# A blocked attention and feed-forward kernel: the second block's attention queued behind the first's, four weight pieces split without ScalarE, and one small operation moved

## The chip, the cores and the metric

The kernel runs on one core of a Trainium2 chip. Such a core has five engines with a queue each, in which instructions run in order: TensorE (PE, with its weight loads PEld), VectorE (DVE), ScalarE (ACT), GpSimd (POOL) and SyncE (SP), which here only issues DMAs. The metric is the device time of one execution in microseconds. A kernel is run several times and the median counts; one execution is recorded by the profiler, and all durations in the text come from it.

## The reference

Attention within chunks of 64 tokens (8 batches, 8 heads, 576 tokens, 64 dimensions), and behind it a feed-forward layer over all 4608 tokens with a parametric ReLU.

```python
scores = scale * np.matmul(q_c, k_c.transpose(0, 1, 2, 4, 3))
scores = scores - np.max(scores, axis=-1, keepdims=True)
attn = np.exp(scores)
attn = attn / (np.sum(attn, axis=-1, keepdims=True) + 1e-09)
x = np.matmul(attn, v_c)          # brought to 4608 x 512
h = x @ w_in                      # 512 -> 2048
g = np.maximum(h, 0.0) + alpha * np.minimum(h, 0.0)
out = g @ w_out                   # 2048 -> 512
```

q, k, v and alpha are float32. The two weight matrices come to the kernel as 64-bit words: they are float64 numbers, and the kernel makes float32 of them with integer operations.

## The kernel before, in words

**Tiling.** A *sub-block* s is 128 tokens: two attention chunks with all 8 heads. There are 36. A *block* b is four sub-blocks (512 tokens). The hidden dimension is cut into 16 *chunks* f of 128. Each chunk has two weight *pieces*, wi[f] and wo[f], of 128 x 512 numbers. Every float32 operand of the feed-forward is split into a high part (the rounded matmul type) and a low part, and three products are added (high with high, low with high, high with low). So the first product of a chunk, `ffn_in` (L305, matmuls at L311), is 12 matmuls of 512 columns, and the second, `ffn_out` (L328, matmuls at L336), is 12 as well.

**Order of phases.** Blocks 0 to 2 go through `ffn_in` and `ffn_out` chunk by chunk; later blocks, in pairs, by another scheme that the change doesn't touch. The first steps are ordered so that the weights need not all be there: phase 0 is block 0 with chunks 0 to 2, phase 1 is block 1 with chunks 0 to 8, phase 2 is block 0 with chunks 3 to 15, and so on (L384). The list `steps` (L462) has an entry n for each (phase, block, chunk).

**Attention of the first two blocks.** Sub-blocks 0 to 7 are "early". `attend(part, s)` (L387) does one of three parts. Part 0 is `attn_scores` (16 matmuls at L178 into a bank ps_a) and `attn_softmax`: on VectorE a maximum (L208) and a scaling (L210), on ScalarE eight exponentials (L215, each with the reading of its sum), then on VectorE L217, a reciprocal (L218) and a multiplication (L219). Part 1 is `attn_transpose`: four transposes on TensorE (L243) and two copies on ScalarE (L250, L251). Part 2 is `attn_values` (16 matmuls at L261) and `attn_x`: ScalarE copies the high part, xh (L293), VectorE makes the low part, xl (L294). `ffn_in` reads the xh and xl of all four sub-blocks of its block, so it starts when the last of them is there. For s below 6 the transposes and the results of part 2 lie in the banks ps_o0 to ps_o3, in which `ffn_out` later sums; for s of 6 and 7 they lie in the two banks ps_a.

**Where it is called.** The parts of sub-blocks 0 to 3 are called in a loop ahead of the steps (L451). Those of sub-blocks 4 to 7 are put into `beside[n]` (L463) and called at the head of the first three steps (L820). All of them carry a raised priority.

**Weight pieces.** `fetch` (L115) loads one piece, 512 KB, into one of three buffers, from SP's queue. `split_weight` (L121) makes a float32 number of each 64-bit word and splits it. L130 takes the sign off the high words on ScalarE (every second 32-bit word is read). L131 to L134 clamp, shift and join on VectorE. L135 writes the high part on ScalarE, and L136 the low part on VectorE. `prepare(f)` (L139) does both pieces of a chunk: chunk 0 ahead of the attention loop, every further chunk in a step. `prepare(f, behind)` puts the instructions that stand on the engine of `behind` after it in that engine's queue. The dictionary at L827 names it: for chunk 2 the low part xl of sub-block 4 (`done_x[4]`), for chunk 3 that of 6, for chunk 4 that of 7.

**What sets the order.** The program order is not the order on an engine. A planner goes through the instructions with their priorities and a model of their durations, and writes each engine's queue at build time; on the chip the queue runs in that order. `tc.issue_after(ins)` fixes one thing for the planner: what is issued within it on the engine of `ins` comes behind `ins` in that engine's queue. It holds nothing on other engines. From step 20 on TensorE's order is the program's own.

**rise.** L448 makes 1 - alpha on VectorE from a small load on POOL's queue (L447). `prelu` (L301) reads it at L303, after the first `ffn_in`.

Of the kernel before, what the change touches and what calls it, by code (L numbers as in the profile page):

```python
# [11 lines left out]
AF = mybir.ActivationFunctionType  # L12
ALU = mybir.AluOpType
# [14 lines left out]
def tile_local_attention_prelu_ffn(  # L28
# [12 lines left out]
    nc = tc.nc  # L41
# [11 lines left out]
    SPB = TB // P  # L53
# [19 lines left out]
    def f32(t):  # L73
        return t.bitcast(F32)
# [31 lines left out]
    def pe(ins):  # L106

        return tc.keep_in_program_order(ins) if pinned[0] else ins

    wi, wo = {}, {}  # L110
# [7 lines left out]
        raws[side, f] = stage.tile([P, 512], I64, name=name, bufs=2 if name == "raw" else 1)  # L118
        nc.sync.dma_start(out=raws[side, f], in_=(w_in if side == "wi" else w_out)[:, f])

    def split_weight(side, f):  # L121
        if (side, f) not in raws:
            fetch(side, f)
        raw = raws.pop((side, f))
        words = raw.bitcast(U32).rearrange("p (n two) -> p two n", two=2)
        low, high = words[:, 0], words[:, 1]
        t1 = stage.tile([P, 512], U32, name="t1")
        w = const.tile([P, 2, 512], F32R, name=f"{side}{f}")
        hi, lo = w[:, 0], w[:, 1]
        nc.scalar.activation(f32(t1), f32(high), AF.Abs)  # L130
        nc.vector.tensor_scalar(f32(t1), f32(t1), bits(0x38000000), bits(0x47EFFFFF), op0=ALU.max, op1=ALU.min)  # L131
        nc.vector.tensor_scalar(t1, t1, 3, 0x3FFFFFF8, op0=ALU.logical_shift_left, op1=ALU.bitwise_and)
        nc.vector.scalar_tensor_tensor(t1, in0=high, scalar=0xC0000000, in1=t1, op0=ALU.bitwise_and, op1=ALU.bitwise_or)
        nc.vector.scalar_tensor_tensor(t1, in0=low, scalar=29, in1=t1, op0=ALU.logical_shift_right, op1=ALU.bitwise_or)  # L134
        nc.scalar.copy(hi, f32(t1))  # L135
        nc.vector.tensor_tensor(lo, f32(t1), f32(hi), op=ALU.subtract)  # L136
        return w

    def prepare(f, behind=None):  # L139
        with tc.issue_after(behind.ins) if behind else nullcontext():  # L140
            wi[f] = split_weight("wi", f)
            wo[f] = split_weight("wo", f)


    att = []
# [108 lines left out]
    def attn_values(s):  # L254
        v_sb = qkv.pop(s)[2]
        p = pdiag.pop(s)
        if s < EARLY:
            xo = attn_psum(s, 2)
            for h in range(H):
                par, hp = h % 2, h // 2  # L260
                pe(nc.tensor.matmul(  # L261
                    xo[par * C:(par + 1) * C, hp * P:(hp + 1) * P],
                    lhsT=v_sb[:, h * C:(h + 1) * C],
                    rhs=p[:, :, h],
                    start=True, stop=True,
                ))
            return xo.rearrange("p (g t) -> p g t", t=P)
# [10 lines left out]
                    ))  # L278
        return [a[:, :NP * C].rearrange("p (g t) -> p g t", t=C) for a in att]

    done_x = {}

    def attn_x(s, xo):
        sl = slice((s % SPB) * P, (s % SPB + 1) * P)
# [5 lines left out]
            return  # L290
        xh, xl = x[s // SPB]
        if s < EARLY:
            nc.scalar.copy(xh[:, :, sl], xo)  # L293
            done_x[s] = nc.vector.tensor_tensor(xl[:, :, sl], xo, f32(xh[:, :, sl]), op=ALU.subtract)  # L294
            return
        for c in range(2):
# [148 lines left out]
    first_v(2)  # L445
    fetch("wi", 1)
    nc.gpsimd.dma_start(out=alpha_sb, in_=alpha)  # L447
    nc.vector.tensor_scalar(rise, alpha_sb, -1.0, 1.0, op0=ALU.mult, op1=ALU.add)  # L448
    prepare(0)
    ready = 1  # L450
    for i in range(SPB + 2):  # L451
        for st in range(2, -1, -1):
            if 0 <= i - st < SPB:
                attend(st, i - st)
                if st == 2 and i % 2:
# [2 lines left out]
                    first_k(i + 2, nc.sync)  # L458
                    first_v(i + 1)


    steps = [(p, b, f) for p, (b, f0, f1) in enumerate(phases) for f in range(f0, f1)]  # L462
    beside = [[] for _ in steps]  # L463
# [336 lines left out]
    for n, (p, b, f) in enumerate(steps):  # L800
# [17 lines left out]
                    dst, src = finals.pop(0)  # L818
                    nc.sync.dma_start(out=dst, in_=src)
        for st, s in beside[n]:  # L820
            attend(st, s)
        if 2 * n in late:
            if 2 * n == visits[0]:
                attn_load(late[2 * n][1], "q")
            visit(*late[2 * n])
        if ready < NF:
            prepare(ready, done_x.get({2: SPB, 3: SPB + 2, 4: SPB + 3}.get(ready)))  # L827
            ready += 1
        elif n in COMBINE:

            with tc.issue_after(stages["softmax"][0].ins), tc.issue_after(stages["softmax"][1].ins):
                combine(*combined.pop(0), 23 <= n <= 36)
# [79 lines left out]
```

## Time and profile before

| what | value |
|---|---|
| median of 3 runs | 832.8 us (831.98 to 834.33) |
| the profiled execution: its own time | 834.16 us |
| its span, first to last instruction | 832.4 us |
| mean granted TensorE clock | 0.993 of full speed |

The profile counts from the span's start. A row of the timeline gives start, duration, engine, line, operation, output and inputs. "x16" says that 16 of a kind are merged in a row, and a bracket names the idle time ahead of it and what ended it. A row of groups gives count, busy us and mean ns of one. Names such as wo or wi in attention rows are the memory that the tile is kept in: before the weights of the last chunks are loaded, their room serves the attention's buffers.

### The profile page before, as it was taken

Reading aid. Unit: us, or ns where it says so; the run is one execution under the profiler, and the core shown is the slowest. Engines: PE = TensorE matmul, PEld = TensorE weight load, DVE = VectorE, ACT = ScalarE, POOL = GpSimd, SP = SyncE. Lnnn points to the kernel's source line nnn. Section 1 sums busy time; section 2 is a strip of 40 time slices with the busy share of each in tenths; the row PEclk is TensorE's granted clock in tenths of the full one; section 3 lists DMA queues with packets and bytes.
Section 4 is the critical chain, followed back from the end, with each engine's and each line's share of the span. In section 5 each row is a group of like instructions: output and inputs, shape, how many; then the busy total and the mean of one; then the engine's idle time right before and its main releaser. Section 6 shows DMA issues by size and latency. Waiting matters only on the chain.

```text
span 832.4 us, 15117 instructions
## 1 busy us (share of the span) xinstructions
PE 805.4 (97%) x5248; PEld 644.8 (77%) x5248; DVE 656.0 (79%) x1177; ACT 465.8 (56%) x1276; POOL 212.4 (26%) x340
## 2 busy tenths in 40 slices
PE   4799999999999999999999999999999999999998
PEld 3568788777777778787888787777887878888886
DVE  5687999987967988577788997777789956668875
ACT  5974565546563756565566554655465533345452
POOL 4006232323433322111112241111122512121232
PEclk9899999999999999999999999999999999999999
DMA  9729889556876767688876899786567995555788
GB/s 279 216 78 326 276 274 321 173 159 203 217 238 155 239 215 255 224 253 272 262 246 201 236 249 330 252 277 202 189 195 247 244 297 182 189 190 186 237 228 234
DMA packets 73964, 192.39 MB, mean 231 GB/s; under 512 B 11664, under 2 KB 19104, under 8 KB 73760
## 3 DMA queue, kind: packets, MB, share of 16 engines
q0 software_dynamic: 38272, 127.43, 49.8%
q1 hardware_dynamic: 27248, 48.91, 18.8%
q10 hardware_dynamic: 8368, 15.08, 5.9%
q8 instruction: 42, 0.69, 0.4%
q14 instruction: 34, 0.28, 0.1%
HBM read 135.27 MB, written 42.99 MB: 214 GB/s over the span
## 4 chain that ended last, share of the span: by engine, by line
PE 84%; DMA 6%; ACT 4%; DVE 4%; issue 1%; SPq 1%; POOL 0%; DVEq 0%; ACTq 0%
PE ps_o L624 19%; PE ps_o L757 15%; PE ps_o L336 12%; PE ps_h L311 12%; PE ps_h L757 12%; PE ps_h L624 9%; PE ps_a L273 2%; PE ps_a L192 1%; DMA raw<-w_in 1%; DMA pT<-t 1%; DMA wi<-qT 1%; DMA more<-w_in 1%; DMA wo_a<-raw 1%; ACT pr L215 1%; SPq L233 1%
## 5 line engine op out<-in xcount | busy, mean ns | idle before, releaser
L336 PE MATMUL ps_o<-wo,gh 128*128 128x512 f32 x384 | 116.4, 396 | 0.1
L311 PE MATMUL ps_h<-xh,wi 128*128 128x512 f32 x384 | 106.1, 400 | 2.6 <-ACT xh L293 2.3
L311 PEld LDWEIGHTS ps_h<-xh,wi 128*128 128x128 f32 x384 | 71.6, 189 | 20.3 <-ACT xh L293 2.5
L336 PEld LDWEIGHTS ps_o<-wo,gh 128*128 128x128 f32 x384 | 71.7, 188 | 17.5 <-ACT gh L323 0.3
L336 PE MATMUL ps_o<-wo,gl 128*128 128x512 f32 x192 | 71.2, 396 | 0.0
L624 PE MATMUL ps_o<-wi,raw 128*128 128x512 f32 x171 | 68.4, 400 | 0.0
L215 ACT ACTIVATE pr<-ps_a,mx 128x64 f32<-128x64 f32 x224 | 67.2, 325 | 0.7
L624 PE MATMUL ps_o<-wo,raw 128*128 128x512 f32 x171 | 67.3, 394 | 0.0
L311 PE MATMUL ps_h<-xl,wi 128*128 128x512 f32 x192 | 53.1, 397 | 0.0
L562 POOL DMA_DIRECT2D raw<-wi_a x42 | 22.3, 532 | 105.1 <-PE ps_o L624 61.8
L215 ACT ACTIVATION_READ_ACCUMULATOR pr<-ps_a,mx 128x1 f32 x224 | 48.8, 218 | 0.0
L302 ACT ACTIVATE wo<-gh 128x512 f32<-128x512 f32 x24 | 15.2, 633 | 52.0 <-DVE gh L647 52.0
L562 POOL DMA_DIRECT2D raw<-wo_a x42 | 22.3, 532 | 84.7 <-PE ps_o L757 43.9
L323 ACT CAST gh<-g 128x512 fp32r<-128x512 f32 x48 | 29.9, 624 | 24.1 <-DVE g L303 15.2
L311 PEld LDWEIGHTS ps_h<-xl,wi 128*128 128x128 f32 x192 | 36.3, 190 | 8.9 <-issue 0.2
L336 PEld LDWEIGHTS ps_o<-wo,gl 128*128 128x128 f32 x192 | 36.0, 188 | 8.7 <-issue 0.2
L580 ACT CAST gh<-wi 128x512 fp32r<-128x512 f32 x45 | 28.0, 622 | 26.2 <-PE ps_o L757 9.3
L324 DVE TENSOR_TENSOR gl<-g,gh 128x512 fp32r<-128x512 f32 x48 | 32.8, 684 | 8.8 <-ACT gh L323 8.5
L302 ACT ACTIVATE g<-ps_h 128x512 f32<-128x512 f32 x48 | 29.2, 608 | 18.8 <-PE ps_h L311 18.7
L303 DVE SCALAR_TENSOR_TENSOR g<-g,rise,ps_h 128x512 f32<-128x512 f32 x48 | 35.6, 741 | 5.0 <-ACT g L302 5.0
L624 PE MATMUL ps_o<-wi,wo 128*128 128x512 f32 x99 | 39.4, 398 | 0.0
L624 PE MATMUL ps_o<-wo,wo 128*128 128x512 f32 x99 | 39.2, 396 | 0.0
(247 smaller groups left out, 2154.6 us busy)
## 6 DMA issues: line engine op xcount, KB each, us to landing
raw<-wi_a POOLq DMA_DIRECT2D x42, 512.0 KB, 4.6
raw<-wo_a POOLq DMA_DIRECT2D x42, 512.0 KB, 4.6
wi<-wi_a POOLq DMA_DIRECT2D x21, 512.0 KB, 4.6
wo<-wi_a POOLq DMA_DIRECT2D x21, 512.0 KB, 4.6
wi<-wo_a POOLq DMA_DIRECT2D x21, 512.0 KB, 4.6
wo<-wo_a POOLq DMA_DIRECT2D x21, 512.0 KB, 4.3
v_sb<-v SPq DMA_DIRECT2D x28, 256.0 KB, 5.1
wi_a<-raw POOLq DMA_DIRECT2D x28, 256.0 KB, 3.5
```

The lines of the kernel that those rows point to most:

```text
L215: last = nc.scalar.activation(pr[:, g], one, AF.Exp, bias=mx[:, g], scale=SCALE, accum_out=sm[:, g])
L273: pe(nc.tensor.matmul(att[c][par * C:(par + 1) * C, hp * C:(hp + 1) * C], lhsT=v_sb[rows, h * C:(h + 1) * C], rhs=p[rows, :, par * NP + hp ...
L302: nc.scalar.activation(g, h, AF.Relu, scale=-1.0)
L303: nc.vector.scalar_tensor_tensor(g, in0=g, scalar=rise[:, f:f + 1], in1=h, op0=ALU.mult, op1=ALU.add)
L311: pe(nc.tensor.matmul(hps, lhsT=wi[f][:, l, k * P:(k + 1) * P], rhs=xx[:, k], start=(i == 0 and k == 0), stop=(i == 2 and k == NK - 1),))
L323: nc.scalar.copy(gh, g)
L324: low = nc.vector.tensor_tensor(gl, g, f32(gh), op=ALU.subtract)
L336: pe(nc.tensor.matmul(o, lhsT=a[:, ts], rhs=wo[f][:, l], start=(f == first and i == 0), stop=(f == last and i == 2),))
L562: streamed[0] = nc.gpsimd.dma_start(out=f32(t), in_=units[side][n])
L580: hi = nc.scalar.copy(t_hi, t)
L624: pe(nc.tensor.matmul(ps, lhsT=w[:, l, k * P:(k + 1) * P], rhs=xx[:, xl], start=first and at == 0, stop=at == n - 1, skip_group_check=not ...
L757: pe(nc.tensor.matmul(ps[m], lhsT=w[:, l, m * P:(m + 1) * P], rhs=xx, start=i != 6 and j == 0 and n == 0, stop=j == JF - 1 and n == 2, ski ...
```

## The change

Four things are done.

1. `split_weight` gets an argument `alone`, true for chunks 0 and 1. With it the sign is taken off by a bitwise AND on VectorE in place of ScalarE's Abs, and the high part is written by a copy on VectorE in place of ScalarE's. The four pieces of these chunks then need no ScalarE.
2. `attn_x` keeps ScalarE's copy in `copied_x[s]`, and `attn_values` its last matmul in `valued[s]`. All parts of sub-blocks 4 to 7 are issued behind `copied_x[3]` on ScalarE and behind `valued[3]` on TensorE, which are the first block's last.
3. The operation for `rise` moves from ahead of `prepare(0)` to after the first attention loop, behind `done_x[0]` on VectorE. Its load stays.
4. `prepare(2)` stands behind `done_x[3]` in place of `done_x[4]`.

```diff
-    def split_weight(side, f):
+    def split_weight(side, f, alone):
...
-        nc.scalar.activation(f32(t1), f32(high), AF.Abs)
+        if alone:
+            nc.vector.tensor_scalar(t1, high, 0x7FFFFFFF, None, op0=ALU.bitwise_and)
+        else:
+            nc.scalar.activation(f32(t1), f32(high), AF.Abs)
...
-        nc.scalar.copy(hi, f32(t1))
+        if alone:
+            nc.vector.tensor_copy(hi, f32(t1))
+        else:
+            nc.scalar.copy(hi, f32(t1))
...
-            wi[f] = split_weight("wi", f)
-            wo[f] = split_weight("wo", f)
+            wi[f] = split_weight("wi", f, f < 2)
+            wo[f] = split_weight("wo", f, f < 2)
...
-                pe(nc.tensor.matmul(
+                valued[s] = pe(nc.tensor.matmul(
...
-            nc.scalar.copy(xh[:, :, sl], xo)
+            copied_x[s] = nc.scalar.copy(xh[:, :, sl], xo)
...
-    nc.vector.tensor_scalar(rise, alpha_sb, -1.0, 1.0, op0=ALU.mult, op1=ALU.add)
     prepare(0)
...
+    with tc.issue_after(done_x[0].ins):
+        nc.vector.tensor_scalar(rise, alpha_sb, -1.0, 1.0, op0=ALU.mult, op1=ALU.add)
...
         for st, s in beside[n]:
-            attend(st, s)
+            with tc.issue_after(copied_x[SPB - 1].ins), tc.issue_after(valued[SPB - 1].ins):
+                attend(st, s)
...
-            prepare(ready, done_x.get({2: SPB, 3: SPB + 2, 4: SPB + 3}.get(ready)))
+            prepare(ready, done_x.get({2: SPB - 1, 3: SPB + 2, 4: SPB + 3}.get(ready)))
```

(`SPB`, sub-blocks per block, is 4.)

2 lines of the change are left out of this document (1 added, 1 removed).

## The prediction

> **What bounds the kernel now.** I read the page first, then the busy time by stretches, then the chain of waits of the first 80 us.
>
> ```profile
> span 832.4 us, 15117 instructions
> ...
> PE 805.4 (97%) x5248; PEld 644.8 (77%) x5248; DVE 656.0 (79%) x1177; ACT 465.8 (56%) x1276; POOL 212.4 (26%) x340
> ```
>
> TensorE is busy 805.4 of 832.4 us, so only 27 us of idle time can be won without taking matmuls away, and the change takes none away. The stretches of 20 us (sums of PE, PEld, DVE, ACT, POOL busy, then the granted clock) show where those 27 us lie.
>
> ```profile
> 0.00:20.00 20.00, 9.26 (x88) 7.35 (x88) 10.51 (x26) 10.48 (x44) 9.00 (x21) 1.00 0.94 280
> 20.00:40.00 20.00, 13.63 (x126) 10.94 (x128) 15.24 (x35) 19.47 (x85) 0.00 (x0) 0.83 0.78 234
> 40.00:60.00 20.00, 18.89 (x124) 14.04 (x118) 16.19 (x34) 14.01 (x46) 0.00 (x0) 1.00 0.17 54
> ...
> 240.00:260.00 20.00, 17.61 (x128) 14.04 (x128) 11.38 (x25) 12.49 (x50) 2.96 (x4) 0.91 0.61 170
> ```
>
> The first 40 us hold 17.1 us of it (20 - 9.26 and 20 - 13.63). In the second of these stretches ScalarE is busy 19.47 of 20: there it is the bound, not TensorE. The chain of waits (start, duration, engine, line) says what ends this stage.
>
> ```profile
> 28.02 1.49 ACT wo L215 x10
> ...
> 33.31 1.48 ACT wo L215 x10
> ...
> 36.16 0.51 ACT wo L135
> 36.66 0.50 ACT xh L293
> ...
> 37.20 2.12 PE ps_h L311 x8
> ```
>
> The first feed-forward matmul (L311) starts at 37.20, when the copy L293 of the first block's last sub-block is done. Ahead of that copy ScalarE runs softmax exponentials (L215) and weight pieces (L135). The first exponentials of sub-block 4, the second block's first, stand in the timeline here, and the copy of its last sub-block, 7, here:
>
> ```profile
> 27.88 0.36 ACT L215 ACTIVATE wo<-ps_a,mx 128x64 f32<-128x64 f32 x1
> ...
> 61.34 0.59 ACT L293 CAST xh<-ps_a 128x512 fp32r<-128x512 f32 x1
> ```
>
> So two sub-blocks of exponentials (4 and 5) that nobody needs yet go ahead of the copy that everybody waits for.
>
> **The change, part by part.** *ScalarE before the first feed-forward matmul.* These are the groups of ScalarE from 13.7 to 37.2 us that belong to weight pieces (count, busy us, mean ns), and one row of the timeline:
>
> ```profile
> L130 ACT ACTIVATE t<-raw 128x512 f32<-128x512 f32 x3 | 2.1, 694 | 0.0
> ...
> L135 ACT CAST wo<-t 128x512 fp32r<-128x512 f32 x2 | 1.3, 666 | 0.0
> ...
> L130 ACT ACTIVATE t<-more 128x512 f32<-128x512 f32 x1 | 0.7, 678 | 0.8 <-DMA more<-w_in 0.8
> L135 ACT CAST wi<-t 128x512 fp32r<-128x512 f32 x1 | 0.6, 643 | 0.0
> ```
> ```profile
> 32.63 0.67 ACT L130 ACTIVATE t<-raw 128x512 f32<-128x512 f32 x1
> ```
>
> The row at 32.63 is a piece of chunk 2, which stays on ScalarE. The other three L130 (2.1 us) and the three L135 (1.9 us) leave. Ten L215 rows, which are five exponentials with their sums, take 1.49 us, so 0.30 us each, and the 16 of sub-blocks 4 and 5 take 4.8 us; they go behind the copy. Together 8.8 us, and ScalarE has next to no idle time there, so the earliest start is 37.2 - 8.8 = 28.4 us.
>
> *What is late next is VectorE.* It takes over an AND and a copy for each of four pieces. The groups of VectorE (13.7 to 64.2 us) bound their price:
>
> ```profile
> L134 DVE SCALAR_TENSOR_TENSOR t<-raw,t 128x512 uint32<-128x512 uint32 x5 | 3.4, 687 | 0.0
> ...
> L131 DVE TENSOR_SCALAR t<-t 128x512 f32<-128x512 f32 x8 | 3.2, 422 | 0.7 <-ACT t L130 0.7
> ```
>
> Eight instructions at 0.42 (one source, like L131) are 3.4 us, at 0.69 (L134, which also reads every second word) 5.5 us. I take 0.42, since both have one source as L131 has, and keep 5.5 for the range. The Trainium skill ("VectorE: DVE Perf Modes", section "The perf-mode tier table (the rule you actually need)") gives fp32 copies and tensor_scalar in SBUF twice the rate of two-source operations, which the 0.42 against 0.69 here bears out for dense operands; no row here shows it for the strided AND. In return VectorE loses the wait of L448:
>
> ```profile
> DVE rise L448 <- DMA alpha_sb<-alpha: 1.2, 1, 1.2
> ```
>
> Now behind done_x[0], some 8 us later in the queue, it finds its load landed and costs nothing there; the 1.2 us came ahead of sub-block 0's reciprocal. Its DMA stays where it was on POOL's queue. Against this, VectorE's queue is in order, and an urgent reduction or reciprocal can stand behind a piece's 0.4 to 0.7 us. With some five such operations for each of sub-blocks 1 to 3, 15 in all, and every third of them behind 0.42 us of a piece, I take 2.1 us (bounds: nothing, and all 5.5 us). The start of L311 becomes 28.4 + 2.1 = **30.5**, 6.7 us earlier.
>
> *TensorE from there.* Rows of the timeline, and one of the chain (12 full matmuls):
>
> ```profile
> 30.58 1.09 PE L261 MATMUL ps_o<-wo,wi 128*64 128x128 f32 x16 [0.67 <-ACT wo L251]
> ...
> 34.26 0.66 PE L243 MATMUL ps_o<-ident,wo 128*128 128x128 f32 x4
> ...
> 61.36 2.14 PE L336 MATMUL ps_o<-wo,gh 128*128 128x512 f32 x8
> ```
> ```profile
> 235.21 2.81 PE ps_h L311 x12
> ```
>
> Phase 0 (block 0, chunks 0 to 2) is six groups of 12 matmuls: 16.8 us. The second block's attention is now wholly behind the start: four times 1.09 + 0.66 + 1.09 = 11.4 us. At best TensorE has done both at 30.5 + 28.2 = 58.7. In before the last group of phase 0 starts at 61.36 (L336) and is worth 2.8, so the same point is 64.2. The ceiling of the gain is 5.5 us, not 6.7, because three score groups and a transpose that lay in idle time now lie in the full stretch.
>
> *The added waits.* All of the second block's ScalarE instructions stand behind copied_x[3], its TensorE ones behind valued[3]. Behind those stand the prelu copies of block 0 on ScalarE, and, through PSUM banks ps_o0 to ps_o3 that sub-blocks 4 and 5 use, the first ffn_out. Until then TensorE has three ffn_in (8.4 us) and scores, so that wait is covered until some 41 us. What decides is when sub-block 7's copy (before: 61.34 + 0.59 = 61.9) lets phase 1 go on. Groups of ScalarE (37.1 to 64.2), and stretches:
>
> ```profile
> L323 ACT CAST gh<-g 128x512 fp32r<-128x512 f32 x3 | 1.9, 617 | 0.1
> ...
> L302 ACT ACTIVATE g<-ps_h 128x512 f32<-128x512 f32 x3 | 1.8, 599 | 3.5 <-PE ps_h L311 3.5
> ```
> ```profile
> 13.70:30.50 16.80, 11.95 (x110) 9.28 (x106) 13.00 (x34) 15.80 (x71) 0.00 (x0) 0.80 1.04 301
> 30.50:37.20 6.70, 3.65 (x52) 3.00 (x52) 4.61 (x12) 6.64 (x30) 0.00 (x0) 1.00 0.67 229
> 37.20:64.20 27.00, 25.62 (x164) 19.46 (x165) 22.01 (x45) 20.02 (x59) 1.42 (x3) 1.00 0.25 79
> ```
>
> VectorE worked 13.00 + 4.61 + 22.01 = 39.6 us from 13.7 to 64.2. Without chunk 3's two pieces (five operations of 0.42 to 0.69, some 2.9 us each, 5.8) and with the added 3.4 it needs 37.2; with the 3.8 us idle that it had up to 30.5, it is through at 13.7 + 37.2 + 3.8 = 54.7, with the dearer AND and copy at 56.8. ScalarE had less to do in the last stretch (20.02 against 22.01). So the copy can come at some 57 at the earliest. At the latest its chain keeps its old length from first exponential to last copy (61.9 - 27.9 = 34.0) from the new start: 64.5. I take the middle, **60.8**: half of the old chain's waits were for sub-block 0 to 3 and weight work that is now gone. TensorE goes on at 60.8 instead of 64.2: **3.4 us won**.
>
> *The rest.* prepare(2)'s VectorE part follows done_x[3] instead of done_x[4]: some 10 instructions, a sub-block earlier; its loads sit on SP's queue and aren't held. They compete with the second block on VectorE, which the 39.6 includes. On SP's queue the loads of values for 4 to 7 wait for TensorE's reads and only come earlier. From 64 us on TensorE is pinned or full, and the shift goes to the end. The 2.4 us idle in 240 to 260 may move by 1.5 us either way, which I cost at nothing and put into the range.
>
> **Sum.** Span 832.4 - 3.4 = 829.0; the profiled execution's own 834.16 becomes 830.8; it lay 1.4 above the median of the runs shown, 832.8, which becomes **829.4**.
>
> **Rivals.** *TensorE's ceiling:* the copy comes before 58.7 and all 5.5 us are won: 827.3. For it speak ScalarE's 20.02 and VectorE's 22.01 of 27 us; against it that both run in order behind one another. *The chain moves whole:* it keeps 34.0 us, ends at 64.5, and 0.3 is lost: 833.1.
>
> ```profile
> 41.47 0.24 ACT L215 ACTIVATION_READ_ACCUMULATOR wi<-ps_a,mx 128x1 f32 x1
> ...
> 52.33 0.32 ACT L215 ACTIVATE wi<-ps_a,mx 128x64 f32<-128x64 f32 x1
> ```
>
> For it speaks that from sub-block 6's last exponential to 7's first 10.6 us went by, while TensorE and VectorE worked through their queues and ScalarE was not the bound. That includes the case that the change doesn't do what it says: ScalarE's freed time fills with chunk 2's pieces. *Slower:* VectorE in the second block's softmax. Each added us there stretches the chain of 34.0; with all 3.4 to 5.5 us in it, the copy comes at 67.9 to 70.0, and the time is 3.7 to 5.8 longer: about 837.5. It decides once the copy comes later than 64.2. For it speaks 22.01 of 27 busy already, against it that four pieces can be split before 30.5 where 3.8 us are idle. *Half clock:*
>
> ```profile
> 20.00:25.00 5.00, 2.28 (x20) 1.88 (x22) 4.76 (x12) 4.96 (x25) 0.00 (x0) 0.71 1.05 284
> 25.00:30.00 5.00, 4.90 (x40) 3.83 (x36) 3.36 (x10) 4.99 (x25) 0.00 (x0) 0.60 1.03 299
> ```
>
> The granted clock is 0.71 and 0.60 after TensorE's idle time: 5 x 0.29 + 5 x 0.40 = 3.4 us lost. If that stretch falls on the new start, TensorE's end goes from 58.7 to 62.1, past 60.8, and 1.3 of the gain is lost: 830.7. The Trainium skill ("TensorE: Matmul & The Clock Gate", section "What's actually happening") has the clock halve after an idle window of about 3.4 us; by that rule one cold window would cost an estimated 1.7 us.
>
> **How the numbers follow.** Forecast 829.4 (own range 828.0 to 831.0): 0.35. Ceiling: 0.18. Whole chain: 0.24. Slower: 0.15. Half clock: 0.08. About 0.3%, 2.5 us, is what a measurement tells from no change: faster is below 830.3, slower above 835.3. Faster gets the ceiling and nearly all of the forecast, 0.53; slower 0.15, the rest is 0.32. The range goes from 826.0 (the ceiling and part of the later wait) to 835.5, which leaves out most of the slower case and little else.
>
> **What would show it.** L130 and L135 appear on ScalarE for chunks 2 and up only; L311 first at 29 to 32; sub-block 7's copy at 59 to 62; VectorE over 90% from 30 to 58; L448 without a wait. I am wrong if L311 starts after 34, if the AND or copy costs over 0.7, or if TensorE stands idle for over 4 us between 31 and 64.

## The result, and the profile after

The changed kernel is slower: 846.44 us (median, 843.52 to 847.09) against 832.39 us (831.89 to 834.33) of the kernel before beside it, a ratio of 1.0158 (95% interval 1.0128 to 1.0187). The forecast was 829.4, with a range up to 835.5. In the profiled executions the span grows from 832.4 to 845.1 us.

The line numbers of the changed kernel are some six higher: Abs is L133, ScalarE's cast of a piece L141, the new AND L131, the new copy L139, the scores L184, the maximum L214, the exponentials L221, xh L299, xl L300, `ffn_in` L317, `ffn_out` L342, prelu L308 and L309, rise L468.

| profiled execution | before | after | forecast |
|---|---|---|---|
| first `ffn_in` matmul | 37.20 | 33.96 | 30.5 |
| first exponential of sub-block 4 | 27.88 | 40.53 | 30.5 |
| first exponential of sub-block 6 | 39.24 | 50.20 | |
| sub-block 7's copy xh starts | 61.34 | 68.99 | some 60.2 (60.8 at its end) |
| span | 832.4 | 845.1 | 829.0 |

The added operations first. Groups of the changed kernel by line and shape, in its first 40 us (count, then busy us and mean ns of one, then the idle time ahead):

```profile
L131 DVE TENSOR_SCALAR t<-raw 128x512 uint32<-128x512 uint32 x3 | 1.3, 439 | 3.8 <-DMA raw<-w_in 3.4 <-DMA raw<-w_out 0.3
...
L139 DVE CAST wi<-t 128x512 fp32r<-128x512 f32 x2 | 0.9, 472 | 0.0
L139 DVE CAST wo<-t 128x512 fp32r<-128x512 f32 x2 | 0.8, 424 | 0.0
...
L468 DVE TENSOR_SCALAR rise<-alpha_sb 128x16 f32<-128x16 f32 x1 | 0.2, 170 | 0.0
```

They cost what they were put at: 0.42 to 0.47 us, and rise waits for nothing. The strided AND costs as little as the dense one-source row of before (0.44 against 0.42). The loss is in the order. Rows of the changed kernel's timeline (start, duration, engine; the bracket is the idle time ahead and what ended it):

```profile
32.63 0.67 ACT L133 ACTIVATE t<-more 128x512 f32<-128x512 f32 x1 [2.48 <-DMA more<-w_out]
...
33.33 0.58 ACT L299 CAST xh<-ps_o 128x512 fp32r<-128x512 f32 x1
33.94 0.69 DVE L300 TENSOR_TENSOR xl<-ps_o,xh 128x512 fp32r<-128x512 f32 x1 [3.52 <-ACT xh L299]
33.96 1.19 PE L317 MATMUL ps_h<-xh,wi 128*128 128x512 f32 x4 [0.87 <-ACT xh L299]
34.55 0.75 DVE L134 TENSOR_SCALAR t<-t 128x512 f32<-128x512 f32 x2
...
37.09 1.28 DVE L214 TENSOR_REDUCE mx<-ps_a 128x8 f32<-128x512 f32 x2
...
40.53 0.32 ACT L221 ACTIVATE wo<-ps_a,mx 128x64 f32<-128x64 f32 x1
...
45.13 1.09 PE L184 MATMUL ps_a<-wo,wi 128*64 128x128 f32 x16 [1.00 <-ACT wo L221]
...
50.20 0.32 ACT L221 ACTIVATE wi<-ps_a,mx 128x64 f32<-128x64 f32 x1
...
68.99 0.59 ACT L299 CAST xh<-ps_a 128x512 fp32r<-128x512 f32 x1 [1.19 <-PE ps_a L267]
...
69.62 3.54 PE L317 MATMUL ps_h<-xh,wi 128*128 128x512 f32 x8 [0.69 <-ACT xh L299]
...
79.67 1.69 PE L317 MATMUL ps_h<-xh,wi 128*128 128x512 f32 x4 [2.65 <-DVE g L309]
```

ScalarE stands idle for 2.48 us ahead of a piece of chunk 2 whose load isn't there, and sub-block 3's copy is queued behind it. VectorE waits 3.52 us for that copy, then does chunk 2's operations before it takes the second block's maxima (37.09). So sub-block 4's exponentials start at 40.53. Sub-block 6's scores (45.13) wait for exponentials: they use the bank that sub-block 4's scores held. Part of the lateness goes through to sub-block 7's copy: 12.7 us at sub-block 4's first exponential, 11.0 at sub-block 6's, 7.7 at the copy.

Up to 64 us TensorE hardly does less by it. Two stretches, 30 to 64 us, of the kernel before and then of the changed one (TensorE, weight loads, VectorE, ScalarE, GpSimd busy us, granted clock, DMA share, GB/s):

```profile
30.00:64.00 34.00, 29.07 (x215) 22.30 (x216) 26.92 (x57) 27.14 (x88) 1.22 (x2) 1.00 0.35 112
```
```profile
30.00:64.00 34.00, 28.41 (x200) 21.14 (x202) 16.84 (x37) 20.38 (x84) 0.00 (x0) 1.00 0.22 74
```

TensorE is busy for 28.41 us against 29.07. VectorE and ScalarE both do much *less*, 16.84 and 20.38 us of 34 against 26.92 and 27.14. Neither became the bound; they wait for each other.

How many feed-forward matmuls are done shows what this is worth. Windows restricted to one line, before: first the rows of `ffn_in` (L311), then those of `ffn_out` (L336); the figure in the first bracket is the number of matmuls.

```profile
0.00:64.00 64.00, 9.90 (x39) 7.36 (x40) 0.95 0.64 193
...
0.00:80.00 80.00, 20.21 (x81) 15.05 (x81) 0.96 0.70 217
...
0.00:64.00 64.00, 8.41 (x32) 5.78 (x32) 0.95 0.64 193
...
0.00:80.00 80.00, 14.91 (x59) 10.98 (x60) 0.96 0.70 217
```

The same of the changed kernel (L317, then L342):

```profile
0.00:64.00 64.00, 8.91 (x36) 6.64 (x36) 0.97 0.57 177
...
0.00:80.00 80.00, 16.63 (x61) 12.51 (x62) 0.96 0.59 187
...
0.00:64.00 64.00, 9.43 (x36) 6.46 (x36) 0.97 0.57 177
...
0.00:80.00 80.00, 9.43 (x36) 6.46 (x36) 0.96 0.59 187
```

By 64 us the two kernels are level: 39 + 32 = 71 and 36 + 36 = 72. The 72 are the whole of phase 0, six groups of 12. The changed kernel had a head start (24 against 8 at 40 us), but phase 0 holds no more work, and what comes next needs block 1's attention. By 80 us it is 140 against 97, 43 behind; at 0.234 us each (2.81 / 12, the chain's row of the prediction) that is 10.1 us. At 100 us the lag is 47, 11.0 us, and later it doesn't grow (47 at 140 us, 41 at 200).

Windows of the changed kernel at that place:

```profile
64.00:68.00 4.00, 1.64 (x22) 1.19 (x20) 2.25 (x6) 3.78 (x10) 0.00 (x0) 1.00 0.60 221
68.00:72.00 4.00, 3.31 (x22) 2.63 (x21) 4.00 (x9) 1.81 (x3) 0.08 (x1) 0.74 0.24 60
72.00:76.00 4.00, 4.00 (x16) 3.15 (x16) 2.84 (x6) 1.35 (x2) 4.00 (x6) 0.83 0.90 335
76.00:80.00 4.00, 1.35 (x6) 0.80 (x5) 3.97 (x8) 2.72 (x5) 4.00 (x6) 1.00 0.95 283
80.00:84.00 4.00, 4.00 (x12) 3.11 (x11) 2.15 (x5) 0.85 (x3) 3.20 (x5) 0.57 0.95 365
```

TensorE is busy for 1.64 of 4 us from 64, then runs at 0.74 and 0.83 of its clock, stands for 2.65 us until VectorE has made g (79.67), and runs at 0.57 after that. The clock alone costs up to 4 x (0.26 + 0.17 + 0.43) = 3.4 us from 68 to 84.

The Trainium skill ("TensorE: Matmul & The Clock Gate", section "What's actually happening") has the gate halve the clock after an idle window of about 3.4 us. The trace agrees that idle time is followed by the slower clock. The idle stretch ahead of the 0.57 is 2.65 us, though, shorter than that window.

### The profile page after: what moved, and what is told of

Its sections match the earlier page's. It is cut to its first block, busy times and chain, and to the rows that moved or that the text cites. A ratio compares the mean times of both kernels' runs of the same rounds, so it can differ in the third digit from the quotient of the medians.

```text
span 845.1 us, 15109 instructions
## 1 busy us (share of the span) xinstructions
PE 810.2 (96%) x5248; PEld 648.2 (77%) x5248; DVE 658.2 (78%) x1185; ACT 462.0 (55%) x1268; POOL 213.2 (25%) x340
## 4 chain that ended last, share of the span: by engine, by line
PE 75%; DMA 8%; DVE 7%; ACT 3%; SPq 3%; issue 2%; POOL 1%; DVEq 0%; ACTq 0%; POOLq 0%
PE ps_o L632 19%; PE ps_o L765 15%; PE ps_h L765 10%; PE ps_o L342 10%; PE ps_h L317 9%; PE ps_h L632 9%; SPq L239 3%; DMA pT<-t 2%; PE ps_a L279 1%; DMA wi_a<-raw 1%; DMA raw<-w_out 1%; PE ps_a L198 1%; DMA raw<-wi_a 1%; DMA more<-w_out 1%; DMA wo_a<-raw 1%
## 5 line engine op out<-in xcount | busy, mean ns | idle before, releaser
L342 PE MATMUL ps_o<-wo,gh 128*128 128x512 f32 x384 | 116.0, 397 | 1.0 <-DVE xl L300 1.0
L317 PE MATMUL ps_h<-xh,wi 128*128 128x512 f32 x384 | 108.4, 409 | 5.5 <-DVE g L309 3.9
L317 PEld LDWEIGHTS ps_h<-xh,wi 128*128 128x128 f32 x384 | 73.3, 194 | 24.3 <-DVE g L309 4.8
L342 PEld LDWEIGHTS ps_o<-wo,gh 128*128 128x128 f32 x384 | 71.6, 188 | 18.6 <-DVE xl L300 1.4
L342 PE MATMUL ps_o<-wo,gl 128*128 128x512 f32 x192 | 70.5, 395 | 0.0
L221 ACT ACTIVATE pr<-ps_a,mx 128x64 f32<-128x64 f32 x224 | 67.1, 324 | 0.7
L317 PE MATMUL ps_h<-xl,wi 128*128 128x512 f32 x192 | 55.8, 406 | 0.0
L570 POOL DMA_DIRECT2D raw<-wi_a x42 | 22.4, 532 | 105.4 <-PE ps_o L632 62.1
L221 ACT ACTIVATION_READ_ACCUMULATOR pr<-ps_a,mx 128x1 f32 x224 | 48.6, 217 | 0.0
L317 PEld LDWEIGHTS ps_h<-xl,wi 128*128 128x128 f32 x192 | 37.5, 195 | 9.1
L308 ACT ACTIVATE wo<-gh 128x512 f32<-128x512 f32 x24 | 15.2, 633 | 52.3 <-DVE gh L655 52.3
L342 PEld LDWEIGHTS ps_o<-wo,gl 128*128 128x128 f32 x192 | 36.1, 188 | 8.6
L588 ACT CAST gh<-wi 128x512 fp32r<-128x512 f32 x45 | 28.0, 621 | 26.3 <-PE ps_o L765 10.2
L309 DVE SCALAR_TENSOR_TENSOR g<-g,rise,ps_h 128x512 f32<-128x512 f32 x48 | 35.5, 740 | 7.0 <-ACT g L308 6.8
L632 PE MATMUL ps_o<-wo,wo 128*128 128x512 f32 x99 | 39.2, 396 | 0.0
L308 ACT ACTIVATE g<-ps_h 128x512 f32<-128x512 f32 x48 | 29.2, 608 | 17.6 <-PE ps_h L317 16.3
```

What stands on the lines that cost most here:

```text
L221: last = nc.scalar.activation(pr[:, g], one, AF.Exp, bias=mx[:, g], scale=SCALE, accum_out=sm[:, g])
L308: nc.scalar.activation(g, h, AF.Relu, scale=-1.0)
L309: nc.vector.scalar_tensor_tensor(g, in0=g, scalar=rise[:, f:f + 1], in1=h, op0=ALU.mult, op1=ALU.add)
L317: pe(nc.tensor.matmul(hps, lhsT=wi[f][:, l, k * P:(k + 1) * P], rhs=xx[:, k], start=(i == 0 and k == 0), stop=(i == 2 and k == NK - 1),))
L342: pe(nc.tensor.matmul(o, lhsT=a[:, ts], rhs=wo[f][:, l], start=(f == first and i == 0), stop=(f == last and i == 2),))
L570: streamed[0] = nc.gpsimd.dma_start(out=f32(t), in_=units[side][n])
```

## The experiments

Each kernel ran beside the kernel before on the same chip, whose median was 832.4 to 834.6 us, so ratios are compared. One table for all. The three times are starts in the profiled execution: sub-block 4's and 6's first exponential and sub-block 7's copy. The last column counts feed-forward matmuls by 80 us, as above.

| kernel | median | ratio to before (95%) | span | s4 | s6 | s7 | by 80 |
|---|---|---|---|---|---|---|---|
| before | 832.39 | | 832.4 | 27.9 | 39.2 | 61.3 | 140 |
| after | 846.44 | 1.0158 (1.0128 to 1.0187) | 845.1 | 40.5 | 50.2 | 69.0 | 97 |
| e1_chunk2_back | 840.87 | 1.0081 (1.0055 to 1.0108) | 839.3 | 38.6 | 47.4 | 65.4 | 116 |
| e2_no_hold | 836.90 | 1.0034 (1.0012 to 1.0057) | 839.3 | 27.7 | 38.6 | 67.2 | 118 |
| e3_pieces_back | 841.18 | 1.0088 (1.0061 to 1.0115) | 839.1 | 41.6 | 53.0 | 69.5 | 106 |
| e4_hold_alone | 839.26 | 1.0061 (1.0029 to 1.0093) | 836.4 | 38.1 | 47.0 | 65.0 | 120 |
| e5_pieces_alone | 833.77 | 0.9995 (0.9967 to 1.0022) | 833.9 | 28.3 | 37.3 | 61.8 | 135 |
| e6_chunk2_alone | 834.64 | 1.0008 (0.9985 to 1.0031) | 832.2 | 27.7 | 39.4 | 63.8 | 139 |
| e7_hold_scalar_only | 841.98 | 1.0091 (1.0066 to 1.0116) | 841.7 | 34.7 | 48.0 | 66.6 | 110 |
| e8_chunk2_last | 843.77 | 1.0125 (1.0053 to 1.0197) | 840.2 | 33.4 | 44.7 | 63.0 | 102 |
| h_s4 | 839.78 | 1.0071 (1.0045 to 1.0097) | 835.5 | 32.9 | 44.2 | 62.8 | 126 |
| h_s5 | 837.27 | 1.0026 (1.0006 to 1.0046) | 834.2 | 28.0 | 39.3 | 61.6 | 139 |
| best1 | 832.91 | 0.9991 (0.9963 to 1.0019) | 833.5 | 24.8 | 37.2 | 60.5 | 143 |
| o_rise | 834.70 | 1.0008 (0.9980 to 1.0035) | 829.7 | 28.7 | 40.0 | 62.1 | 137 |
| a_s4_free | 838.02 | 1.0049 (1.0026 to 1.0072) | 837.2 | 26.8 | 43.4 | 64.2 | 126 |
| best1_pool | 835.90 | 1.0024 (1.0002 to 1.0045) | 831.8 | 26.3 | 39.8 | 61.6 | 140 |

In the kernels that hold or move several sub-blocks, the exponentials of two of them can be interleaved; "s6" is then good to 2 us or so.

### One part of the change undone

**e1_chunk2_back**, the changed kernel with

```diff
-            prepare(ready, done_x.get({2: SPB - 1, 3: SPB + 2, 4: SPB + 3}.get(ready)))
+            prepare(ready, done_x.get({2: SPB, 3: SPB + 2, 4: SPB + 3}.get(ready)))
```

> The changed kernel, with chunk 2's pieces again behind the low part of sub-block 4 (done_x[4]) as before; all else as changed. Theory CHUNK (chunk 2's eight VectorE operations at 33.9 to 39.5 us stand ahead of the second block's reductions and scalings): the first exponentials of sub-block 4 come at 35 to 37 us instead of 40.5, sub-block 7's copy some 4 us earlier than 69.0, and the time falls by 4 to 9 us, to 837 to 842. Theory HOLD (the second block starts too late because everything of it stands behind the first block's last copy): sub-block 7's copy stays within 2 us of 69.0 and the time within 3 us of 846. Theory LOAD (VectorE has too much to do with the four pieces): no difference either.

**e2_no_hold**, the changed kernel with

```diff
-            with tc.issue_after(copied_x[SPB - 1].ins), tc.issue_after(valued[SPB - 1].ins):
-                attend(st, s)
+            attend(st, s)
```

> The changed kernel without the hold: the second block's attention is free on ScalarE and TensorE, as before; pieces on VectorE alone, the later 1 - alpha and chunk 2 behind done_x[3] stay. HOLD: the exponentials of sub-blocks 4 and 5 go into ScalarE's idle time between 20 and 33 us (9 us idle there in the changed kernel), sub-block 7's copy comes at 56 to 62, and the time is 829 to 834. CHUNK: chunk 2's pieces still stand ahead of work of the second block, so 838 or more. LOAD: 838 or more as well, since the pieces stay on VectorE.

**e3_pieces_back**, the changed kernel with

```diff
-            wi[f] = split_weight("wi", f, f < 2)
-            wo[f] = split_weight("wo", f, f < 2)
+            wi[f] = split_weight("wi", f, False)
+            wo[f] = split_weight("wo", f, False)
```

> The changed kernel with all weight pieces again split by ScalarE and VectorE together; hold, later 1 - alpha and chunk 2 behind done_x[3] stay. LOAD: eight operations of 0.43 us (3.4 us) leave VectorE and the time falls by 3 us or more, to 843 or less. HOLD and CHUNK: VectorE was not full between 40 and 64 us, so nothing is won; ScalarE gets six conversions of 0.65 back ahead of the first block's last copy, and the time is 844 to 850.

**e4_hold_alone**, the kernel before with the hold of sub-blocks 4 to 7 on ScalarE and TensorE only:

```diff
-            attend(st, s)
+            with tc.issue_after(copied_x[SPB - 1].ins), tc.issue_after(valued[SPB - 1].ins):
+                attend(st, s)
```

> The kernel before with nothing but the hold added: sub-blocks 4 to 7 behind the first block's last copy on ScalarE and its last matmul on TensorE. HOLD: sub-block 7's copy comes at 65 us or later and the time is 840 to 846. CHUNK: the hold alone costs little, 831 to 836. LOAD: as CHUNK.

Measured: without the hold 0.34% is left of the 1.58%; without the early chunk 2 0.81%, without the pieces on VectorE 0.88%. The hold by itself costs 0.61%. So the hold is the largest single part, but no part carries all of it. Against what was expected: e1 has CHUNK's time and earlier copy, but its exponentials came at 38.6, not at 35 to 37. e2 lies between the theories, above HOLD's 829 to 834 and below the others' 838. e3 has LOAD's 843 or less, though the pieces cost nothing alone (e5 below). e4 has HOLD's copy at 65.0, and its time lies 0.7 us under HOLD's 840 to 846.

Without the hold (e2) sub-block 6's exponentials are back at 38.6 us, yet sub-block 7's copy is still late. Rows of e2's timeline:

```profile
64.16 1.10 PE L267 MATMUL ps_a<-wi,wi 128*64 128x128 f32 x16 [0.32 <-ACT wi L257]
64.77 0.59 ACT L372 COPY wo<-ps_o 128x512 f32<-128x512 f32 x1
...
66.73 0.61 ACT L372 COPY wi<-ps_o 128x512 f32<-128x512 f32 x1
67.20 0.62 ACT L299 CAST xh<-ps_a 128x512 fp32r<-128x512 f32 x1
```

The values end at 65.3, but ScalarE's queue has four copies of block 0's sums (L372) and a piece's cast ahead of the urgent xh. The planner ordered them so; on the chip it costs 2 us. e2's profiled execution was also its slowest (841.12 against a median of 836.90), so its trace shows more loss than is usual for e2.

### Parts alone, and the hold on one engine

**e5_pieces_alone** and **e6_chunk2_alone** are the kernel before with one part each:

```diff
-            wi[f] = split_weight("wi", f)
-            wo[f] = split_weight("wo", f)
+            wi[f] = split_weight("wi", f, f < 2)
+            wo[f] = split_weight("wo", f, f < 2)
```
```diff
-            prepare(ready, done_x.get({2: SPB, 3: SPB + 2, 4: SPB + 3}.get(ready)))
+            prepare(ready, done_x.get({2: SPB - 1, 3: SPB + 2, 4: SPB + 3}.get(ready)))
```

> The kernel before with nothing but the four pieces of chunks 0 and 1 on VectorE alone; no hold, chunk 2 behind done_x[4], 1 - alpha early. LOAD (VectorE's added work costs by itself): slower than before by 3 us or more, 837 and up. RELIEF (ScalarE is the bound of the first 37 us and this frees it): the first block's last copy comes earlier than 36.5 us and the time is 829 to 833. ORDER (what each engine's queue comes to is what counts, and the freed time is filled with other work of the second block): the first copy not earlier than 36.5, the time 833 to 838.

> The kernel before with nothing but chunk 2 behind done_x[3] in place of done_x[4]. If chunk 2's early place costs by itself: 837 or more, with sub-block 7's copy at 64 us or later. If it costs only together with the hold, which puts the second block's reductions at that very place: 831 to 836 and the copy at 60 to 63, since sub-blocks 4 and 5 are reduced before 30 us here.

**e7_hold_scalar_only** is the changed kernel with the hold on ScalarE alone and chunk 2 back at `done_x[4]`; **e8_chunk2_last** is e7 with chunks 2 and 3 later:

```diff
-            with tc.issue_after(copied_x[SPB - 1].ins), tc.issue_after(valued[SPB - 1].ins):
+            with tc.issue_after(copied_x[SPB - 1].ins):
...
-            prepare(ready, done_x.get({2: SPB, 3: SPB + 2, 4: SPB + 3}.get(ready)))
+            prepare(ready, done_x.get({2: SPB + 2, 3: SPB + 3, 4: SPB + 3}.get(ready)))
```

> The changed kernel with the hold on ScalarE alone (TensorE free to make the second block's scores early) and chunk 2 behind done_x[4] again. If the hold costs by the scores and reductions that come late (TensorE's half of it): sub-block 4's exponentials start within 1.5 us of the first block's last copy, sub-block 7's copy comes before 61 us, and the time is 828 to 834. If it costs by ScalarE's idle time that can't be used: the copy still comes at 64 us or later and the time is 837 to 841, like the changed kernel with chunk 2 put back (840.9).

> As the run before this one, but chunk 2's VectorE part behind the low part of sub-block 6 and chunk 3's behind that of 7, so that no weight piece stands among the second block's softmax. LATE (the time follows sub-block 7's copy): the copy at 52 to 58 us and the time 826 to 832, the best of all. WEIGHTS (the pieces are then late for phase 0's third chunk and for phase 1): TensorE waits over 4 us for chunk 2, and the time is 834 or more.

Measured: the pieces and the early chunk 2 alone change nothing that can be told (0.9995 and 1.0008). In e5 sub-block 3's copy even comes at 41.36, later than before's 36.49, for the planner fills ScalarE's freed time with the second block's exponentials. The hold on ScalarE alone (e7) is as dear as that on both engines (1.0091 against e1's 1.0081, intervals overlapping), so the loss is not TensorE's hold. With TensorE free sub-block 4's exponentials do come 3.9 us earlier (34.7 against e1's 38.6), right behind sub-block 3's copy, but sub-block 7's copy doesn't (66.6 against 65.4). e8 takes the pieces out of the way: sub-block 4's exponentials come at 33.4, 7 us earlier than in the changed kernel, sub-block 7's copy at 63.0, and it still costs 1.25%. Two of e8's windows:

```profile
56.00:60.00 4.00, 1.09 (x4) 0.72 (x4) 2.58 (x7) 2.04 (x12) 0.00 (x0) 0.77 0.00 0
60.00:64.00 4.00, 3.02 (x19) 2.45 (x20) 3.90 (x8) 2.53 (x5) 0.00 (x0) 0.50 0.18 30
```

TensorE is dry there: by 56 us 48 of the 72 matmuls of phase 0 are done, by 64 only 51. Phase 0 now lacks chunk 2. The copy of sub-block 7 alone therefore does not tell the time; what TensorE has done by 80 us does.

Of the expectations, ORDER came for e5. e6 has the time of its second case (831 to 836), with the copy 0.8 us past that case's 63. e7 has the early exponentials of its first case, but the copy and the loss of its second, 1 us above that range. For e8 WEIGHTS came; LATE's copy at 52 to 58 didn't.

### Which sub-block's hold

**h_s4** and **h_s5** are the kernel before with the hold on ScalarE, and for one sub-block:

```diff
-            attend(st, s)
+            with tc.issue_after(copied_x[SPB - 1].ins) if s == SPB else nullcontext():
+                attend(st, s)
```

(h_s5 has `s == SPB + 1`.)

> The kernel before, with the hold on ScalarE alone (behind copied_x[3]) and for sub-block 4 alone; pieces, chunk 2 and rise as before. Theory (sub-block 4's bank): sub-block 4's exponentials come some 10 us later than before (35 to 39 in place of 28), its scores keep their ps_a bank until then, so sub-block 6's exponentials come at 44 or later (before 39.2) and sub-block 7's copy at 64 or later (before 61.3): 4 us or more slower, 837 to 841. Rival (idle ScalarE: what costs is ScalarE time that stays unused ahead of the first feed-forward matmul, whichever sub-block is held): half of what the whole hold costs, +2 to +3, 835 to 837, and sub-block 6's exponentials at 41 to 43. Rival (the hold costs by the cold TensorE only): the granted clock between 24 and 40 is below 0.7 and the time follows it, not the copy.

> The kernel before, with the hold on ScalarE alone and for sub-block 5 alone; sub-block 4 is free. Theory (sub-block 4's bank): sub-block 4's exponentials stay ahead of sub-block 3's copy at 27 to 31, sub-block 6's come at 39 to 42, sub-block 7's copy at 60 to 63; time 831 to 836, not over 0.3% from before. Sub-block 3's copy may come 1 to 4 us earlier than at 36.6. Rival (idle ScalarE): +2 to +3, 835 to 837, with sub-block 7's copy at 63 to 66. If sub-block 6's exponentials come at 44 or later here too, the bank that sub-block 5's scores hold does the same, and sub-block 4 is nothing special.

Rows of h_s4's timeline:

```profile
32.88 0.32 ACT L221 ACTIVATE wo<-ps_a,mx 128x64 f32<-128x64 f32 x1
...
37.80 1.10 PE L317 MATMUL ps_h<-xh,wi 128*128 128x512 f32 x4
...
38.83 1.09 PE L184 MATMUL ps_a<-wo,wi 128*64 128x128 f32 x16
...
44.23 0.31 ACT L221 ACTIVATE wi<-ps_a,mx 128x64 f32<-128x64 f32 x1
```

And of h_s5's:

```profile
28.02 0.34 ACT L221 ACTIVATE wo<-ps_a,mx 128x64 f32<-128x64 f32 x1
...
34.10 1.04 PE L184 MATMUL ps_a<-wo,wi 128*64 128x128 f32 x16
...
35.75 0.32 ACT L221 ACTIVATE wo<-ps_a,mx 128x64 f32<-128x64 f32 x1
...
39.28 0.31 ACT L221 ACTIVATE wi<-ps_a,mx 128x64 f32<-128x64 f32 x1
```

Holding sub-block 4 alone costs 0.71%, 5.9 us, as much as the whole hold (0.61%). Its profiled execution ran at a granted clock of 1.00 from 24 to 100 us and took 837.31 us. The kernel before beside it took 830.3 to 835.5 us, 833.8 on average, in its five executions with a mean clock of 0.998 or more. So some 3.5 us are lost without a slower TensorE clock. The rest of the 5.9 may be the clock's: four of h_s4's six executions, with means of 0.993 to 0.997, took 839.7 to 841.8. Of the theory's numbers sub-block 6's 44 or later and the time came; the exponentials of 4 (32.9 for 35 to 39) and sub-block 7's copy (62.8 for 64 or later) came earlier than it had them. Holding 5 alone costs 0.26%, at the edge of what can be told: sub-block 6's exponentials stay at 39.3, as the theory had it, but the time, 837.3, is over its 831 to 836 and at the rival's +2 to +3, though not with the rival's copy at 63 to 66 (it came at 61.6). In h_s4 sub-block 5's exponentials too run behind 4's (from 35.2), so it holds both in effect. One thing of the theory isn't borne out there: sub-block 6's scores don't wait for the bank in h_s4. They stand in TensorE's queue behind 24 matmuls of `ffn_in`, and sub-block 6's exponentials stand in ScalarE's queue behind the copies and casts of 4 and 5. The bank's wait itself shows only where TensorE is held as well: 1.00 us in the changed kernel (at 45.13), 1.60 in e3, 0.34 in e1 and e4; whether the planner put those scores late because of the bank wasn't tried.

**o_rise** is the kernel before with the later operation:

```diff
-    nc.vector.tensor_scalar(rise, alpha_sb, -1.0, 1.0, op0=ALU.mult, op1=ALU.add)
     prepare(0)
...
+    with tc.issue_after(done_x[0].ins):
+        nc.vector.tensor_scalar(rise, alpha_sb, -1.0, 1.0, op0=ALU.mult, op1=ALU.add)
```

> The kernel before with the later 1 - alpha alone. VectorE doesn't wait 1.2 us for alpha's load ahead of sub-block 0's reciprocal. All theories: no effect that lasts, as the first two blocks' end is set later; sub-block 7's copy at 60 to 63, time 831 to 836. If it is over 2.5 us slower, the later place of this operation is part of what the changed kernel loses, and the sums of the other parts must be taken again.

1.0008, no effect that can be told, as expected.

### Sub-block 4 free in the changed kernel, and two tries for a faster one

**a_s4_free**, the changed kernel with

```diff
-            with tc.issue_after(copied_x[SPB - 1].ins), tc.issue_after(valued[SPB - 1].ins):
-                attend(st, s)
+            if s == SPB:
+                attend(st, s)
+            else:
+                with tc.issue_after(copied_x[SPB - 1].ins), tc.issue_after(valued[SPB - 1].ins):
+                    attend(st, s)
```

> The changed kernel with one thing undone: sub-block 4 isn't held, neither on ScalarE nor on TensorE; sub-blocks 5 to 7 are, chunk 2 stands behind done_x[3], the pieces and rise as changed. Theory (sub-block 4's bank): its exponentials go back ahead of sub-block 3's copy (25 to 31), sub-block 6's come at 37 to 43 in place of 50.2, sub-block 7's copy at 59 to 64 in place of 69.0; 831 to 837. Rival (chunk 2's pieces: their VectorE operations ahead of the second block's reductions are worth some 5 us by themselves, as the changed kernel lost 5.6 us more than the one with chunk 2 put back): 838 to 842, and sub-block 6's exponentials at 44 or later. Rival (hold of sub-blocks 5 to 7): 843 or more.

Freeing this one sub-block takes the ratio from 1.0158 to 1.0049, some two thirds of the loss. Three rows of its timeline:

```profile
26.80 0.31 ACT L221 ACTIVATE wo<-ps_a,mx 128x64 f32<-128x64 f32 x1
...
38.19 1.28 DVE L214 TENSOR_REDUCE mx<-ps_a 128x8 f32<-128x512 f32 x2
...
41.02 0.32 ACT L221 ACTIVATE wo<-ps_a,mx 128x64 f32<-128x64 f32 x1
```

The exponentials of 4 are early again (26.80), but the maxima of 5 and 6 come at 38.19, behind chunk 2's pieces, and sub-block 7's copy at 64.15. The time, 838.0, is above the theory's range by 1 us and at the low end of the rival's. So sub-block 4's hold is the greater part of the loss. That the early chunk 2, which costs nothing alone, is part of what is left is what the maxima's place suggests.

**best1** keeps the pieces and rise as changed, holds sub-block 5 alone on ScalarE, and has chunk 2 back at `done_x[4]`:

```diff
-            with tc.issue_after(copied_x[SPB - 1].ins), tc.issue_after(valued[SPB - 1].ins):
+            with tc.issue_after(copied_x[SPB - 1].ins) if s == SPB + 1 else nullcontext():
                 attend(st, s)
...
-            prepare(ready, done_x.get({2: SPB - 1, 3: SPB + 2, 4: SPB + 3}.get(ready)))
+            prepare(ready, done_x.get({2: SPB, 3: SPB + 2, 4: SPB + 3}.get(ready)))
```

> The changed kernel with three things undone: sub-block 4 isn't held, the hold on TensorE is gone, and chunk 2 stands behind done_x[4] again. Left are the pieces of chunks 0 and 1 on VectorE alone, the later rise, and the hold of sub-block 5 on ScalarE. Theory (sub-block 4's bank): sub-block 3's copy at 33 to 36 and sub-block 7's at 59 to 63: 829 to 835, level with before or a little faster. Rival (idle ScalarE): with 8.8 us gone from ScalarE's queue more of it stays unused, 837 to 841, as with the hold and the pieces together (841 to 842).

**best1_pool** is best1 with a part of the pieces' work on GpSimd:

```diff
-        nc.vector.tensor_tensor(lo, f32(t1), f32(hi), op=ALU.subtract)
+        eng = nc.gpsimd if 3 <= f < 9 and side == "wo" else nc.vector
+        eng.tensor_tensor(lo, f32(t1), f32(hi), op=ALU.subtract)
```

> The kernel of best1 with the low part of the pieces wo of chunks 3 to 8 written by GpSimd in place of VectorE (six operations). best1 was 3 feed-forward matmuls ahead of before at 80 us and 1 behind at 100, where VectorE was busy 3.7 to 4 of 4 us. Theory (VectorE sets the pace from 80 to 100): six operations of 0.69 us leave VectorE's queue, 4 us in all, of which 0.5 to 2 us come through to TensorE: 829 to 833. Rival (GpSimd is late: its operation takes 2 us or more, and ffn_out of the chunk and the DMA issues behind it wait): 834 to 842.

best1 is level with before (0.9991), as its theory had it. It differs from e7 in one thing only, that sub-blocks 4, 6 and 7 aren't held, and e7 costs 0.91%. Sub-blocks 6 and 7 lie behind sub-block 3's copy in before too (39.24 against 36.49), so this leaves sub-block 4. best1 has sub-block 3's copy at 33.92 and sub-block 7's at 60.48, and is 3 matmuls ahead at 80 us, but 1 behind at 100 (223 against 224). best1_pool, 1.0024, is no better. Groups of its GpSimd and VectorE from 60 to 100 us, each from a view of its own engine:

```profile
L143 POOL TENSOR_TENSOR wo<-t,wo 128x512 fp32r<-128x512 f32 x5 | 7.7, 1544 | 60.1 <-ACT wo L141 60.1
...
L143 DVE TENSOR_TENSOR wi<-t,wi 128x512 fp32r<-128x512 f32 x5 | 3.7, 731 | 0.7 <-ACT wi L141 0.7
```

The subtraction takes 1.54 us on GpSimd against 0.73 on VectorE. Neither theory was borne out in full: TensorE is full in every window from 64 to 96 us, and the median still isn't lower. No kernel here beats the one before.

## Why the prediction was wrong

*Prices.* AND 0.44, copy 0.42 to 0.47, rise without a wait, L133 and L141 on ScalarE for chunks 2 and up only: as forecast. The early chunk 2 and the later rise cost nothing that can be told by themselves (e6, o_rise): right too. The pieces don't win anything either (e5), though the prediction took 4.0 us off ScalarE for them. One reading was off without harm: the 0.69 that it set against 0.42 for dense operands is L134's, which reads every second word; the dense subtraction L136 takes 0.69 too.

*Start of `ffn_in`: 30.5 forecast, 33.96 measured.* 3.2 of the 6.7 us came. The 8.8 us taken off ScalarE left room, but ScalarE's queue then had a piece of chunk 2 ahead of sub-block 3's copy, and waited 2.48 us for its load. But the load is not the only bound. Rows of e8, where the same piece waits for 0.55 us:

```profile
31.75 1.09 PE L267 MATMUL ps_o<-wi,wi 128*64 128x128 f32 x16 [1.26 <-ACT wi L257]
32.25 0.67 ACT L133 ACTIVATE t<-more 128x512 f32<-128x512 f32 x1 [0.55 <-DMA more<-w_out]
32.95 0.59 ACT L299 CAST xh<-ps_o 128x512 fp32r<-128x512 f32 x1
```

The copy starts 0.11 us after sub-block 3's last values are there (31.75 and 1.09). In h_s4 it starts at 32.40, 0.05 after them, with all pieces still on ScalarE; no run brings it earlier. So with the second block's exponentials out of the way the first block's own chain of transposes, copies and values sets the start. The prediction subtracted 8.8 us of ScalarE's work and didn't ask when that chain would be done.

*"At the latest its chain keeps its old length from first exponential to last copy (61.9 - 27.9 = 34.0) from the new start: 64.5."* **This step failed.** The length was no underestimate: from 40.53 to 69.58 (68.99 and 0.59) the chain took 29.1 us. Its start was wrong by 10 us, and part of that, 4.9 us, came back in a shorter chain. The prediction let sub-block 4's exponentials start with `ffn_in` at 30.5; they started 10 us later: behind the copy at 33.33, and behind maxima that came at 37.09, behind chunk 2's VectorE operations. Those operations had been counted as busy time ("which the 39.6 includes") and not as a place in an in-order queue: VectorE waited 3.52 us for the copy with chunk 2 lined up behind it, and the maxima behind that. In e1 chunk 2 is out of the way and the exponentials still start at 38.6, since the hold on TensorE puts the scores at 33.6 to 37.1 there; with that gone too they start right behind the copy (e7, 34.7). Their start alone is not the whole loss, for e7 still costs 0.91%. In before, the exponentials of 4 and 5 lay ahead of sub-block 3's copy from 27.9 to 36, in slots of ScalarE that the hold forbids. h_s4 shows that giving up these slots for sub-block 4, and in effect for 5, is enough for 5.9 us; best1, which gives up only 5's, loses nothing.

*"TensorE's ceiling" of 5.5 us.* It treated a head start as a gain. In e5 the first `ffn_in` matmul comes 4.8 us later than before, and the time is the same (0.9995):

```profile
42.00 2.13 PE L317 MATMUL ps_h<-xh,wi 128*128 128x512 f32 x8 [0.66 <-ACT xh L299]
```

So the start of `ffn_in`, which the prediction set out to move, doesn't set the time there. e8 and the changed kernel show the same: phase 0 is 72 matmuls, the changed kernel was 16 ahead at 40 us and level by 64, and from there only block 1's attention counts. That wait the prediction did count, at 60.8; it came at 69.6.

*What was missing in kind:* the price of a late copy. The prediction charged each microsecond of lateness once. The changed kernel's first matmuls of block 1 run at a lower clock (8 of them in 3.54 us; 8 at full clock take 2.12 in the prediction's chain), then TensorE waits 2.65 us for VectorE's g, and runs at 0.57 afterwards. Two windows of e3 at the same place:

```profile
76.00:80.00 4.00, 2.32 (x11) 1.87 (x11) 4.00 (x8) 2.70 (x5) 3.30 (x5) 1.00 1.03 403
80.00:84.00 4.00, 4.00 (x19) 3.25 (x18) 4.00 (x9) 2.24 (x5) 3.06 (x5) 1.00 1.01 376
```

TensorE waits less there, and the clock stays at 1.00. One reason may be that e3 still has 11 matmuls of phase 0 to do at 64 us (61 done against 72), which fill the wait for block 1. e3 is level with the changed kernel at 72 us (80 matmuls against 78) and 15 ahead at 88 (140 against 125); that difference, 3.5 us, comes after the late copy. That the cause is VectorE's order of chunk 3's pieces against prelu is what the rows suggest; it wasn't tried by itself.

*Rivals.* The slower one, at 0.15, had the place of the copy right (67.9 to 70.0; 69.6 measured at its end), but by luck: its mechanism, added work on VectorE, didn't come (VectorE was busy for 16.84 of 34 us), and its price, 837.5, was too low. Nor does the loss begin only once the copy ends after 64.2: e8's ends at 63.6. *Chain moves whole*, at 0.24, moved it from the wrong start. *Half clock* came, not at the new start but after the second dry stretch. Of the things that would show the forecast wrong, TensorE's idle time between 31 and 64 came true: 33.00 - 27.61 = 5.4 us. Before had 4.4 in the same stretch. VectorE, forecast over 90% busy from 30 to 58, was busy for 15.43 of 28 us.

**What stays open.** Hold, pieces and early chunk 2 cost 0.61, nothing and nothing alone; hold with one of the others 0.81 and 0.88 (each with the later rise), all together 1.58. The trace names the waits of the last step, but no run isolates why the parts cost more together than each alone, nor why the copy of sub-block 7 is late in e7 although sub-block 4 starts early. Every edit also goes through the planner anew, so no run moves one place in the queues alone (e5's copy of sub-block 3 moved by 4.9 us). Why h_s5 is 0.26% slower while its count by 80 us is that of before isn't known. Profiled executions differ from medians by up to 4.2 us (e2's 841.12 against 836.90), so counts of one execution explain differences of 5 us, not of 2.

## What to carry to other kernels

When a stage is put first and another queued behind it, ask what the first engine will do when the favoured stage's work is used up: a head start on a stage of fixed size was worth nothing here, as the stage after it was made later. Idle-looking slots ahead of a wait can be the second stage's only early place; a hold gives them up, and all that is chained through banks and in-order queues behind it slips too (here 12.7 us at its start and 7.7 at its end). Add work to an in-order queue as a place (what stands behind it, and from when) and not as busy time.

## What the runs showed that was not expected

The number of feed-forward matmuls done by 80 us goes with the whole run's length: over the fifteen changed kernels, the lag behind before's 140 times 0.234 us agrees with the difference of the spans within 3.4 us (after 10.1 against 12.7, e3 8.0 against 6.7, e4 4.7 against 4.0, h_s4 3.3 against 3.1), while sub-block 7's copy does not (e8 63.0 and 7.8 longer, e6 63.8 and 0.2 shorter). Executions of one kernel on one chip spread by up to 10 us (e2 831.76 to 841.12; best1 828.05 to 838.49), though each engine's queue has the same order every time. The granted clock goes with it: its mean was 0.998 and 0.990 in these two of e2, 1.000 and 0.995 in these two of best1.
